# Stores on GpSimd's queue, and turned 1/sum in one transfer

## The chip, the cores and the metric

The kernel runs on one core of one Trainium2 chip. The metric is the device time of one execution in microseconds (us), as the median of three runs. Before the change it is 641.95 us (641.51 to 647.74). Engines are named as in the profile: PE is TensorE (PEld its weight loads), DVE is VectorE, ACT is ScalarE, POOL is GpSimd, SP is SyncE, which here only issues transfers.

## The reference

Causal attention over 4 batches, 12 heads, 448 positions and 64 columns per head, and behind it two matrix products with ELU between them, over 1792 tokens, 768 model columns and 2048 inner ones. The weights come in as float64 words.

```python
scores = np.matmul(q, k.transpose(0, 1, 3, 2)) / np.sqrt(64)
scores = np.where(mask, -1e9, scores)            # mask: later positions
attn = np.exp(scores - scores.max(-1, keepdims=True))
attn = attn / (attn.sum(-1, keepdims=True) + 1e-9)
x = np.matmul(attn, v)                            # to [1792, 768]
h = x @ w_in
g = np.where(h > 0, h, np.exp(np.minimum(h, 0)) - 1)
out = g @ w_out
```

## The kernel before

Positions are cut in four chunks of 112 (CP); a row tile holds one chunk of all four batches, 448 columns (S). Heads go in six pairs (NP). Work runs in this sequence. For chunk 0, `first_pair` does the attention of each pair. Then `layers(0)` and `layers(1)` take chunks 0 and 1 through the first matrix product, while the attention of chunk 1 and of chunks 2 and 3 (`attention(0)`, `attention(1)`) is mixed into PE's work in lumps. Chunks 2 and 3 go through both products with fewer multiplications: `mixed_h` and `mixed_o` work on sums and differences of blocks, of the weights too. Each product of 32 bit numbers is made as three (`three`), from a high part and a low part that `hi_lo` splits off.

Weights go through DRAM. `load64` loads float64 words, `convert` makes float32 of them with DVE, ACT, DVE, ACT and at the end an addition on POOL (L639), and stores the result to `kin` or `kout` (L650). `fetch` loads it again (L655), `raw_piece` too (L823). `mixed` makes the sums and differences of weights (L675) and stores them to `sin` (L692) or `sout` (L701).

The attention divides by the row sums only after the product with v. `reciprocals` makes 1/sum with positions on partitions, and it is wanted along the free axis, on all partitions of a head. `spread_out` does that: a DVE transpose gives `turned` (tile tt, L403), four small transfers store it to `rdram` (L408, 1 KB each), two transfers load it back, each broadcast over the 64 partitions of a head (L411, tile R), and `scaled_x` multiplies (L388, tile xs). This is done 18 times. For chunks 2 and 3 xs is stored to `xdram` (L394) and loaded when `mixed_h` begins (L850).

Nothing runs in the order in which the code stands. `Plan` collects all work with an engine, a cost and the buffers that it reads and writes, gives each a due time from the back, and then simulates the engines to fix the order on each; where a work may run on DVE, ACT or POOL (`hi_lo`, `add`, `take`), the same simulation chooses. All transfers are issued by SP, in one order, and an SP instruction that waits holds back all behind it. What the planner takes a transfer for is in `dma`: issue time on SP, and a size in us for which the transfer occupies the engines.

Of the kernel before, what the change touches and what calls it, by code (L numbers as in the profile page):

```python
# [9 lines left out]
F32 = mybir.dt.float32  # L10
# [4 lines left out]
ALU = mybir.AluOpType  # L15
AX = mybir.AxisListType

CP = 112
# [219 lines left out]
def attention_moe_kernel(ctx, tc, qk, v, w_in, w_out, out):  # L238
    nc = tc.nc
    B, H, D, _, S = qk.shape  # L240
    FT, P, KT, _ = w_in.shape
    ET = w_out.shape[0]
    NCH = S // CP
    NP = H // 2
# [6 lines left out]
    dram = ctx.enter_context(tc.tile_pool(name="dram", bufs=1, space=bass.MemoryType.DRAM))  # L251
# [5 lines left out]
        out=ident, in_=ident, pattern=[[-1, CP]], compare_op=ALU.not_equal,  # L257
# [5 lines left out]
        out=mask[:, S - CP:], in_=mask[:, S - CP:], pattern=[[-1, CP]], compare_op=ALU.is_ge,  # L263
# [3 lines left out]
    def f32(ap):  # L267
        return ap.bitcast(F32)
# [5 lines left out]
    plan = Plan()  # L274
    rings = {}
    PLACES = dict(
        q=2, k=3, v=5, a=8, at=5, m=2, ob=2, R=2, tt=2, row=47, w6=8, w=7, nm=4, su=4, rr=4, hp=3, p=4, av=1, bank=0,
# [8 lines left out]
    def ring(tag):  # L286
        if tag not in rings:
            long = tag[0] == "w"
            rings[tag] = Heap(PLACES[tag], long) if tag in HEAPS else Ring(PLACES[tag], tag != "p", long)
        return rings[tag]  # L290

    def new(tag, shape, dtype=F32, name=None):
        pool = ps if tag in BANKS else sb
        slot = "row" if tag in ROWS else "bank" if tag in BANKS else tag
        bufs = SHARED.get(slot) or PLACES[slot]
        return ring(tag).new(lambda: pool.tile(shape, dtype, tag=slot, name=name or tag, bufs=bufs))
# [4 lines left out]
    def act(n, fn, more=0.05):  # L301
        return ("ACT", more + 0.84e-3 * n, fn, False)

    def dve(n, fn, rate=1.05e-3, more=0.08, port=False):
        return ("DVE", more + rate * n, fn, port)
# [1 line left out]
    def pool(n, fn, rate=2.3e-3):  # L307
        return ("POOL", 0.1 + rate * n, fn, True)

    def dma(kb, rows, fn, reads, writes, least=0.0):  # L310
        rate = 16.0 / (15.0 * rows / (kb * 1024.0) + 0.0366)
        plan.add(("SP", 0.35 + 0.5e-3 * rows, fn, False), reads, writes, size=max(least, kb / rate))

    xt = {}
    xf = {}
    xdram = dram.tile([NP, 2, P, S], F32, name="xdram")
    rdram = dram.tile([3, NP, 2 * B, P], F32, name="rdram")
    xkept = {}  # L320

    def done(*bufs):
# [6 lines left out]
    def half_of(half):  # L329
        return slice(half * D, (half + 1) * D)  # L330
# [49 lines left out]
        )  # L380
        xt[g, p] = xh, xl

    def blocks(x):
        return x.rearrange("p (x c) -> p x c", x=B)

    def scaled_x(joint, j, av, r):
        x = new("ob", [P, S], name="xs")
        plan.add(dve(S, lambda: nc.vector.tensor_tensor(  # L388
            out=blocks(x()), in0=blocks(av()), in1=r()[:, :, :CP], op=ALU.mult,
        )), [av, r], [x])  # L390
        if joint:
            p, y = divmod(j, 2)
            k = xkept[p, y] = Buf(None, lambda: xdram[p, y])
            dma(224, P, lambda: nc.sync.dma_start(out=k(), in_=x()), [x], [k])  # L394
            return
        xh, xl = row("xh", F32R), row("xl", F32R)
        hi_lo(xh, xl, x, S, xh, xl, x)
        xt[1, j] = xh, xl

    def spread_out(joint, j, rr):  # L400
        home = rdram[joint + j % 2, j // 2] if joint else rdram[0, j]
        k, turned, r = Buf(None, lambda: home), new("tt", [P, 32]), new("R", [P, B, P])
        plan.add(dve(32, lambda: nc.vector.transpose(  # L403
            out=turned(), in_=rr().unsqueeze(1).to_broadcast([P, 4, 2 * B])
        ), more=0.12), [rr], [turned])
        for i in range(4):
            c = slice(32 * i, 32 * i + 32)
            dma(1, 2 * B, lambda i=i, c=c: nc.sync.dma_start(out=home[:, c], in_=turned()[32 * i:32 * i + 2 * B]), [turned], [(k, i)], 0.3)  # L408
        for half in range(2):
            src = home[half * B:(half + 1) * B].rearrange("(o x) q -> o (x q)", o=1).to_broadcast([D, B * P])  # L410
            dma(128, D, lambda half=half, src=src: nc.sync.dma_start(  # L411
                out=r()[half_of(half)].rearrange("p x q -> p (x q)"), in_=src
            ), [k], [(r, half)])
        return r

# [206 lines left out]
    def convert(key):  # L622
        r, w = words.pop(key), new("w", [P, KT, P])
        n = KT if key[0] == "i" else 4
        size = n * P
        low, high = (lambda: r()[:, :n, :, 0]), (lambda: r()[:, :n, :, 1])
        wf = lambda: w()[:, :n]
        plan.add(dve(size, lambda: nc.vector.tensor_scalar(
            wf(), f32(high()), MOST, -MOST, op0=ALU.min, op1=ALU.max
        ), 0.55e-3, 0.06, True), [(r, 1)], [w])  # L630

        plan.add(act(size, lambda: nc.scalar.activation(wf(), wf(), AF.Prelu, scale=REBIAS, alpha=2.0 ** 32)), [], [w])
        plan.add(dve(size, lambda: nc.vector.tensor_scalar(  # L633
            wf().bitcast(U32), wf().bitcast(U32), 3, None, op0=ALU.logical_shift_left
        ), 0.55e-3, 0.06, True), [], [w])
        plan.add(act(size, lambda: nc.scalar.activation(
            low().bitcast(I32), low(), AF.Copy, scale=2.0 ** -29
        )), [], [(r, 0)])
        plan.add(pool(size, lambda: nc.gpsimd.tensor_tensor(  # L639
            out=wf().bitcast(I32), in0=wf().bitcast(I32), in1=low().bitcast(I32), op=ALU.add  # L640
        )), [(r, 0)], [w])
        if key[0] == "i":
            done(r)
            home, src = kin[key[1]], wf
        else:
            h = key[1] // HALF_E
            home = kout[key[1]].rearrange("p (h f) c -> p h f c", h=2)[:, h:, 2 * key[2]:2 * key[2] + 2]
            src = lambda: wf().rearrange("p (h f) c -> p h f c", h=2)[:, h:]
        k = kept[key] = Buf(None, lambda: home)
        dma(n * 64, P, lambda: nc.sync.dma_start(out=home, in_=src()), [w], [k])  # L650
        return w if key[0] == "i" else (w, r)

    def fetch(f):
# [10 lines left out]
    def hi_lo(h, l, x, n, th, tl, tx):  # L664

        plan.add([
            act(n, lambda: nc.scalar.activation(h(), x(), AF.Copy)),  # L667
            dve(n, lambda: nc.vector.tensor_copy(h(), x()), 0.55e-3, 0.06, True),
        ], [tx], [th])
        sub = lambda eng: lambda: eng.tensor_tensor(out=l(), in0=x(), in1=f32(h()), op=ALU.subtract)  # L670
        plan.add([dve(n, sub(nc.vector), port=True), pool(n, sub(nc.gpsimd))], [tx, th], [tl])
# [6 lines left out]
    def mixed(layer, r, x, wa, wb, into=None):  # L678


        h = HALF_K if layer == 1 else 2
        n = h * P
        blk = lambda w, half: lambda: w()[:, half * h:half * h + h]
        a, b = (lambda half: blk(wa, half)), (lambda half: blk(wb, half))
        k = skept[layer, r, x] = Buf(None, lambda: None)
        if layer == 1:
            add(b(1), b(0), b(1), n, ALU.add, [(wb, 0)], [(wb, 1)])
            add(b(0), a(0), b(0), n, ALU.subtract, [(wa, 0)], [(wb, 0)])
            add(a(0), b(1), a(0), n, ALU.subtract, [(wb, 1)], [(wa, 0)])
            add(a(1), a(1), a(0), n, ALU.subtract, [(wa, 0)], [(wa, 1)])  # L690
            for i, w in enumerate((wa, wb)):
                dma(2 * h * 64, 2 * P, lambda i=i, w=w: nc.sync.dma_start(  # L692
                    out=sin[r][:, :, i], in_=w().rearrange("p (h k) c -> p h (k c)", h=2)
                ), [w], [(k, i)])
            return
        m = lambda i: lambda: f32(into().rearrange("p k c w -> p (k c w)"))[:, i * n:i * n + n].rearrange("p (k c) -> p k c", k=h)
        add(m(3), b(0), b(1), n, ALU.add, [wb], [(into, 3)])
        add(m(1), a(0), b(0), n, ALU.subtract, [(wa, 0), (wb, 0)], [(into, 1)])
        add(m(0), m(3), a(0), n, ALU.subtract, [(wa, 0), (into, 3)], [(into, 0)])
        add(m(2), a(1), m(0), n, ALU.subtract, [(wa, 1), (into, 0)], [(into, 2)])  # L700
        dma(4 * h * 64, 4 * P, lambda: nc.sync.dma_start(  # L701
            out=sout[x, :, :, :, r].rearrange("p h i c -> p (h i) c"),
            in_=f32(into().rearrange("p k c w -> p (k c w)"))[:, :4 * n].rearrange("p (m c) -> p m c", m=4),
        ), [into], [k])

    def three(acc, w, k, x, first, last, more=False):
        _, wh, wl = w
# [67 lines left out]
    rows, banks = ring("row"), ring("bank")  # L775

    def row(name, dtype=F32):
        return new("row", [P, S], dtype, name)
# [249 lines left out]
    t = FIRST + EACH * NP + 4.0  # L1028
# [61 lines left out]
```

## Time and profile before

| | us |
|---|---|
| median of 3 runs | 641.95 |
| profiled execution, its own time | 641.22 |
| its span | 639.4 |
| PE busy | 611.0 |
| DVE busy | 514.6 |
| ACT busy | 429.5 |
| POOL busy | 170.1 |

The span runs from the first to the last instruction on the device. Busy time counts computing instructions; issuing a transfer is not counted. A busy PE need not be at its peak, since matmuls overlap and their ends are modelled. The chain of waits follows the end back in time: at each step to what released the instruction, or to the one before it on its engine. What waits for several things is put down to the last.

### The profile page before, as it was taken

Reading aid. Unit: us, or ns where it says so; the run is one execution under the profiler, and the core shown is the slowest. Engines: PE = TensorE matmul, PEld = TensorE weight load, DVE = VectorE, ACT = ScalarE, POOL = GpSimd, SP = SyncE. Lnnn points to the kernel's source line nnn. Section 1 sums busy time; section 2 is a strip of 40 time slices with the busy share of each in tenths; the row PEclk is TensorE's granted clock in tenths of the full one; section 3 lists DMA queues with packets and bytes.
Section 4 is the critical chain, followed back from the end, with each engine's and each line's share of the span. In section 5 each row is a group of like instructions: output and inputs, shape, how many; then the busy total and the mean of one; then the engine's idle time right before and its main releaser. Section 6 shows DMA issues by size and latency. Waiting matters only on the chain.

```text
span 639.4 us, 11598 instructions
## 1 busy us (share of the span) xinstructions
PE 611.0 (96%) x3960; PEld 513.0 (80%) x3960; DVE 514.6 (80%) x1112; ACT 429.5 (67%) x954; POOL 170.1 (27%) x124
## 2 busy tenths in 40 slices
PE   5799999998989899998999999999999999999997
PEld 4655577887878787787888878999999879999996
DVE  5777788589999878897999798597777999997611
ACT  6899887878887886975768675445545766664300
POOL 2145541154345342561322420020001362000000
PEclk9799999999989899999999999999999999999999
DMA  9999997796988999996986677873343233352121
GB/s 213 297 333 334 302 369 217 205 304 203 332 256 280 308 314 292 310 280 224 299 264 217 189 264 229 255 191 117 102 122 99 99 104 95 124 151 67 30 57 43
DMA packets 105819, 135.71 MB, mean 212 GB/s; under 512 B 41120, under 2 KB 76192, under 8 KB 105760
## 3 DMA queue, kind: packets, MB, share of 16 engines
q1 hardware_dynamic: 105760, 134.98, 69.2%
q8 instruction: 31, 0.51, 0.3%
q14 instruction: 28, 0.23, 0.1%
HBM read 103.02 MB, written 31.92 MB: 211 GB/s over the span
## 4 chain that ended last, share of the span: by engine, by line
PE 57%; DVE 14%; DMA 13%; ACT 9%; issue 4%; SPq 2%; DVEq 0%; ACTq 0%
PE op L709 9%; PE op L711 9%; PE op L710 9%; PE hp L709 5%; PE hp L731 5%; PE hp L711 5%; PE hp L710 5%; ACT a L338 4%; DMA w<-kin 4%; PE tr L581 3%; PE av L560 3%; DVE a L334 3%; PE sc L527 2%; DMA qk<-in_qk 2%; DVE whl L670 2%
## 5 line engine op out<-in xcount | busy, mean ns | idle before, releaser
L667 ACT ACTIVATE whl<-w 128x768 fp32r<-128x768 f32 x96 | 80.6, 842 | 80.8 <-PE op L711 49.1
L670 DVE TENSOR_TENSOR whl<-w,whl 128x768 fp32r<-128x768 f32 x100 | 106.3, 1063 | 25.2 <-ACT whl L667 24.5
L709 PE MATMUL op<-ph,whl 128*128 128x448 f32 x336 | 125.7, 374 | 0.0
L711 PE MATMUL op<-ph,whl 128*128 128x448 f32 x336 | 123.2, 367 | 0.0
L710 PE MATMUL op<-pl,whl 128*128 128x448 f32 x336 | 123.2, 367 | 0.0
L338 ACT ACTIVATE a<-a,nm 112x448 f32<-112x448 f32 (+2 forms) x192 | 96.8, 518 | 25.9 <-DVE nm L334 25.6
L639 POOL TENSOR_TENSOR w<-w,w 128x512 int32<-128x512 int32 (+1 forms) x40 | 67.5, 1692 | 118.9 <-DVE w L633 81.0
L334 DVE CUSTOM_DVE_ANT_0 a<-sc,mask 112x448 f32<-112x448 f32 (+2 forms) x192 | 74.2, 443 | 12.9 <-PE sc L438 7.5
L709 PEld LDWEIGHTS op<-ph,whl 128*128 128x128 f32 x336 | 63.1, 188 | 9.3 <-issue 3.5
L711 PEld LDWEIGHTS op<-ph,whl 128*128 128x128 f32 x336 | 63.1, 188 | 5.8
L710 PEld LDWEIGHTS op<-pl,whl 128*128 128x128 f32 x336 | 63.2, 188 | 5.2
L709 PE MATMUL hp<-ph,whl 128*128 128x448 f32 x168 | 61.8, 368 | 1.7 <-DVE u L795 1.6
L711 PE MATMUL hp<-ph,whl 128*128 128x448 f32 x168 | 61.4, 366 | 0.0
L710 PE MATMUL hp<-pl,whl 128*128 128x448 f32 x168 | 61.4, 366 | 0.0
L709 PE MATMUL hp<-xh,whl 128*128 128x448 f32 x144 | 57.7, 401 | 0.0
L711 PE MATMUL hp<-xh,whl 128*128 128x448 f32 x144 | 53.4, 371 | 0.9 <-DVE whl L670 0.9
L710 PE MATMUL hp<-xl,whl 128*128 128x448 f32 x144 | 53.1, 369 | 0.0
L581 PE MATMUL tr<-ident,a 112*112 112x112 f32 x432 | 49.9, 264 | 2.4 <-DVE nm L334 2.3
L560 PEld LDWEIGHTS av<-at,v 112*64 112x64 f32 x864 | 41.6, 137 | 12.4 <-issue 7.7
L560 PE MATMUL av<-at,v 112*64 112x112 f32 x864 | 49.4, 263 | 0.3 <-DVE G L802 0.3
L581 PEld LDWEIGHTS tr<-ident,a 112*112 112x112 f32 x432 | 41.3, 133 | 8.9 <-DVE nm L334 3.2
L585 ACT ACTIVATE at<-tr 112x448 f32<-112x448 f32 (+1 forms) x105 | 46.1, 504 | 2.1 <-PE tr L581 2.0
(113 smaller groups left out, 1123.4 us busy)
## 6 DMA issues: line engine op xcount, KB each, us to landing
w<-kin SPq DMA_DIRECT2D x44, 384.0 KB
w<-in_w_in SPq DMA_DIRECT2D x16, 768.0 KB
w<-in_w_out SPq DMA_DIRECT2D x24, 512.0 KB
w<-sout SPq DMA_DIRECT2D x32, 384.0 KB
w<-kout SPq DMA_DIRECT2D x24, 384.0 KB
qk<-in_qk SPq DMA_DIRECT2D x24, 336.0 KB
kin<-w SPq DMA_DIRECT2D x16, 384.0 KB
sout<-w SPq DMA_DIRECT2D x12, 512.0 KB
```

Of the source, the lines that this page charges most:

```text
L334: plan.add(dve(n, lambda: nc.vector.tensor_tensor_reduce(out=a()[:, c], in0=sc()[:, c], in1=mask[:, S - n:], op0=ALU.add, op1=ALU.min, sca ...
L338: plan.add(act(n, lambda: nc.scalar.activation(a()[:, c], a()[:, c], AF.Exp, bias=nm()[:, x:x + 1], scale=-1.0, accum_out=su()[:, x:x + 1] ...
L560: nc.tensor.matmul(av()[half_of(half), chunk(u % 4)], o["v"][1](half, i), at()[:, chunk(x)], start=i == 0, stop=i == chunks(u) - 1,)
L581: nc.tensor.transpose(tr()[:, chunk(x)], o["a"][half]()[:, chunk(i)], ident)
L585: act(w, lambda: nc.scalar.activation(at()[:, :w], tr()[:, :w], AF.Copy)),
L639: plan.add(pool(size, lambda: nc.gpsimd.tensor_tensor(out=wf().bitcast(I32), in0=wf().bitcast(I32), in1=low().bitcast(I32), op=ALU.add)), ...
L667: act(n, lambda: nc.scalar.activation(h(), x(), AF.Copy)),
L670: sub = lambda eng: lambda: eng.tensor_tensor(out=l(), in0=x(), in1=f32(h()), op=ALU.subtract)
L709: nc.tensor.matmul(acc(), wh(k), xh(), start=first, stop=False, skip_group_check=more)
L710: nc.tensor.matmul(acc(), wh(k), xl(), start=False, stop=False, skip_group_check=more)
L711: nc.tensor.matmul(acc(), wl(k), xh(), start=False, stop=last, skip_group_check=more)
L731: pe(ONE, lambda: nc.tensor.matmul(hp(), w[0]()[:, k], x(), start=k == 0, stop=k == KT - 1), [*w, x], [hp], due)
```

## The change

All stores but those of the results go out from POOL's queue instead of SP's: weights (kin, kout), their sums (sin, sout), xs, and turned 1/sum. The latter goes in one transfer of the whole tile of 128 x 32 instead of four of 8 x 32, and rdram has the layout of that tile. So it comes back in four runs of 512 B per partition instead of one of 2048 B, R is laid out as 4 x 4 x 32, and the product with it is made in two instructions, of 96 and 16 columns per batch. The planner's costs change too: 1.0 us of POOL for a store, 0.36 or 0.57 us of SP for a load, and another formula for the size. Loads and the stores of results stay on SP.

```diff
-    def dma(kb, rows, fn, reads, writes, least=0.0):
-        rate = 16.0 / (15.0 * rows / (kb * 1024.0) + 0.0366)
-        plan.add(("SP", 0.35 + 0.5e-3 * rows, fn, False), reads, writes, size=max(least, kb / rate))
+    def dma(kb, rows, fn, reads, writes, least=0.0, store=False):
+        size = rows * (15.7 + 39.2 * kb / rows) / 16.0e3
+        eng = "POOL" if store else "SP"
+        call = (lambda: fn(nc.gpsimd)) if store else fn
+        plan.add((eng, 1.0 if store else 0.36 if rows <= 128 else 0.57, call, False), reads, writes, size=max(least, size))
...
-    rdram = dram.tile([3, NP, 2 * B, P], F32, name="rdram")
+    rdram = dram.tile([3, NP, P, 32], F32, name="rdram")
...
     def scaled_x(joint, j, av, r):
         x = new("ob", [P, S], name="xs")
-        plan.add(dve(S, lambda: nc.vector.tensor_tensor(
-            out=blocks(x()), in0=blocks(av()), in1=r()[:, :, :CP], op=ALU.mult,
-        )), [av, r], [x])
+        for lo, hi in ((0, 3), (3, 4)):
+            n = min(CP, 32 * hi) - 32 * lo
+            w = min(n, 32)
+            part = lambda t, lo=lo, n=n: t.rearrange("p (x c) -> p x c", x=B)[:, :, 32 * lo:32 * lo + n]
+            cut = lambda t, w=w, part=part: part(t).rearrange("p x (k c) -> p x k c", c=w)
+            plan.add(dve(B * n, lambda lo=lo, hi=hi, w=w, cut=cut: nc.vector.tensor_tensor(
+                out=cut(x()), in0=cut(av()), in1=r()[:, lo:hi, :, :w].rearrange("p k x c -> p x k c"), op=ALU.mult,
+            )), [av, r], [(x, lo)])
...
-            dma(224, P, lambda: nc.sync.dma_start(out=k(), in_=x()), [x], [k])
+            dma(224, P, lambda eng: eng.dma_start(out=k(), in_=x()), [x], [k], store=True)
...
-        k, turned, r = Buf(None, lambda: home), new("tt", [P, 32]), new("R", [P, B, P])
+        k, turned, r = Buf(None, lambda: home), new("tt", [P, 32]), new("R", [P, 4, B, 32])
...
-        for i in range(4):
-            c = slice(32 * i, 32 * i + 32)
-            dma(1, 2 * B, lambda i=i, c=c: nc.sync.dma_start(out=home[:, c], in_=turned()[32 * i:32 * i + 2 * B]), [turned], [(k, i)], 0.3)
+        dma(16, P, lambda eng: eng.dma_start(out=home, in_=turned()), [turned], [k], store=True)
         for half in range(2):
-            src = home[half * B:(half + 1) * B].rearrange("(o x) q -> o (x q)", o=1).to_broadcast([D, B * P])
-            dma(128, D, lambda half=half, src=src: nc.sync.dma_start(
-                out=r()[half_of(half)].rearrange("p x q -> p (x q)"), in_=src
+            src = home.rearrange("(o k r) c -> o k r c", o=1, k=4)[:, :, half * B:(half + 1) * B].rearrange("o k r c -> o k (r c)")
+            dma(128, 4 * D, lambda half=half, src=src: nc.sync.dma_start(
+                out=r()[half_of(half)].rearrange("p k x c -> p k (x c)"), in_=src.to_broadcast([D, 4, B * 32])
             ), [k], [(r, half)])
...
-        dma(n * 64, P, lambda: nc.sync.dma_start(out=home, in_=src()), [w], [k])
+        dma(n * 64, P, lambda eng: eng.dma_start(out=home, in_=src()), [w], [k], store=True)
...
```

The stores to `sin` and `sout` in `mixed` are changed in the same way as that in `convert`. Lines of the changed kernel stand two further down (L408 is L410, L639 is L641).

The planner then gives another order on all engines. On SP, the stretch near the last loads of v (L487, now L489), before:

```order
L655 DMA w<-kin 128x768 x2
L408 DMA rdram<-tt 8x32 x4
L823 DMA w<-kout 128x3x256
L487 DMA v<-in_v 112x512
L394 DMA xdram<-xs 128x448
L655 DMA w<-kin 128x768
L411 DMA R<-rdram 64x512 x2
L692 DMA sin<-w 256x1x384
L655 DMA w<-kin 128x768
L692 DMA sin<-w 256x1x384
L823 DMA w<-sout 128x768
L823 DMA w<-kout 128x3x256
```

and now:

```order
L657 DMA w<-kin 128x768 x2
L489 DMA v<-in_v 112x512
L825 DMA w<-kout 128x3x256
L657 DMA w<-kin 128x768
L413 DMA R<-rdram 64x4x128 x2
L657 DMA w<-kin 128x768
L825 DMA w<-sout 128x768
L489 DMA v<-in_v 112x512
L657 DMA w<-kin 128x768
L825 DMA w<-kout 128x3x256
L657 DMA w<-kin 128x768
L825 DMA w<-sout 128x768
```

The stores rdram (L408), xdram (L394) and sin (L692) no longer stand between the loads; w is a weight tile, R the broadcast 1/sum.

On POOL, around the conversion of the third pair of w_out's tiles, before (w_1313 is its buffer of float64 words):

```order
L639 TENSOR_TENSOR w<-w,w_1313 128x512
L675 TENSOR_TENSOR w_1313<-w 128x256
L639 TENSOR_TENSOR w<-w,w_1719 128x512
L670 TENSOR_TENSOR pl<-G,ph 128x448
L670 TENSOR_TENSOR qkhl<-qk,qkhl 128x672
L639 TENSOR_TENSOR w<-w,w_1818 128x512
L639 TENSOR_TENSOR w<-w,w_1695 128x512
```

and now (there the buffer is w_1272):

```order
L641 TENSOR_TENSOR w<-w,w_1272 128x512
L652 DMA kout<-w 128x256
L672 TENSOR_TENSOR pl<-G,ph 128x448 x2
L641 TENSOR_TENSOR w<-w,w_1691 128x512
L410 DMA rdram<-tt 128x32
L652 DMA kout<-w 256x1x256
L672 TENSOR_TENSOR whl<-w,whl 128x768
L703 DMA sout<-w_1272 512x1x256
L672 TENSOR_TENSOR pl<-G,ph 128x448
L641 TENSOR_TENSOR w<-w,w_1813 128x512
L652 DMA kout<-w 256x1x256
L641 TENSOR_TENSOR w<-w,w_1616 128x512
```

Between the additions of the conversions (L639, now L641) now stand stores of kout (L652), rdram (L410) and sout (L703); a subtraction w<-w (L675) is gone to DVE here, and one of whl has come to POOL. Over the whole program 506 transfers on SP become 354, and POOL gets 98. POOL has three subtractions of whl in place of eight, and DVE 105 in place of 100.

## Rows read from the trace of the kernel before

**Rows 1.** The page: span, engines, DMA queue, chain of waits.

```profile
span 639.4 us, 11598 instructions
...
PE 611.0 (96%) x3960; PEld 513.0 (80%) x3960; DVE 514.6 (80%) x1112; ACT 429.5 (67%) x954; POOL 170.1 (27%) x124
...
q1 hardware_dynamic: 105760, 134.98, 69.2%
...
PE 57%; DVE 14%; DMA 13%; ACT 9%; issue 4%; SPq 2%; DVEq 0%; ACTq 0%
```

**Rows 2.** Windows: length, then busy us and count per engine, granted clock, DMA share, GB/s.

```profile
45.00:400.00 355.00, 343.28 (x2553) 275.26 (x2552) 309.54 (x695) 278.71 (x645) 131.88 (x86) 0.99 0.86 273
140.00:400.00 260.00, 248.28 (x1945) 209.30 (x1942) 237.97 (x510) 197.34 (x452) 94.39 (x63) 0.99 0.85 268
98.00:252.00 154.00, 146.28 (x1115) 121.36 (x1115) 134.82 (x324) 124.73 (x293) 60.71 (x43) 0.98 0.87 270
180.00:220.00 40.00, 36.56 (x263) 30.65 (x264) 37.05 (x88) 30.77 (x68) 16.78 (x12) 0.91 0.93 295
```

**Rows 3.** Waits: engine line <- releaser: us in total, times, longest.

```profile
PE sc L527 <- DVE G L802: 3.3, 2, 2.7
...
DVE w L675 <- DMA w<-kin: 3.5, 2, 3.2
...
ACT qkhl L667 <- DMA qk<-in_qk: 7.0, 4, 3.6
```

**Rows 4.** One line's transfers on SP: issue time ns min/median/max, first and last start.

```profile
L408 SPq DMA_DIRECT2D rdram<-tt x72: 263/292/710, 53.0 to 383.3; - x72
...
L650 SPq DMA_DIRECT2D kin<-w x16: 325/448/1243, 44.6 to 107.1; - x16
```

**Rows 5.** Timeline of SP: start, us, line, transfer, count.

```profile
103.65 1.47 SPq L408 DMA_DIRECT2D rdram<-tt  x4
...
335.84 0.32 SPq L655 DMA_DIRECT2D w<-kin  x1
...
340.31 1.29 SPq L408 DMA_DIRECT2D rdram<-tt  x4
```

**Rows 6.** Chain of waits, in order: start us, us, what.

```profile
107.14 0.55 SPq L650
...
108.87 7.42 DMA R<-rdram
...
127.66 2.20 DMA rdram<-tt
...
148.67 1.15 DMA rdram<-tt
...
165.20 6.85 DMA sout<-w
...
172.12 3.06 DMA kout<-w
...
346.00 4.53 DMA sin<-w
...
350.55 5.54 DMA w<-kout
```

**Rows 7.** Groups of DVE by form: count | busy, mean ns | idle before.

```profile
L670 DVE TENSOR_TENSOR whl<-w,whl 128x768 fp32r<-128x768 f32 x100 | 106.3, 1063 | 25.2 <-ACT whl L667 24.5
...
L334 DVE CUSTOM_DVE_ANT_0 a<-sc,mask 112x448 f32<-112x448 f32 x48 | 27.9, 617 | 3.6 <-PE sc L527 3.5
...
L334 DVE CUSTOM_DVE_ANT_0 a<-sc,mask 112x112 f32<-112x112 f32 x48 | 9.9, 267 | 7.5 <-PE sc L438 7.5
...
L628 DVE TENSOR_SCALAR w<-w 128x512 f32<-128x512 f32 x24 | 15.0, 630 | 4.0 <-DMA w<-in_w_out 2.3 <-POOL whl L670 1.7
```

**Rows 8.** Groups of POOL by form, same columns.

```profile
L639 POOL TENSOR_TENSOR w<-w,w 128x768 int32<-128x768 int32 x16 | 31.2, 1954 | 43.5 <-DVE w L633 26.1 <-ACT w L636 8.1 <-DMA kin<-w 3.1
...
L675 POOL TENSOR_TENSOR w<-w 128x256 f32<-128x256 f32 x5 | 5.0, 1008 | 0.3
```

More of the change, by code (lines that the diff above doesn't have):

```diff
@@ L381, in split_x @@
         xt[g, p] = xh, xl
-    def blocks(x):
-        return x.rearrange("p (x c) -> p x c", x=B)
     def scaled_x(joint, j, av, r):
         x = new("ob", [P, S], name="xs")
-        plan.add(dve(S, lambda: nc.vector.tensor_tensor(
-            out=blocks(x()), in0=blocks(av()), in1=r()[:, :, :CP], op=ALU.mult,
-        )), [av, r], [x])
+        for lo, hi in ((0, 3), (3, 4)):
[6 more added lines that the diff above has]
+            )), [av, r], [(x, lo)])
         if joint:
@@ L691, in mixed @@
             for i, w in enumerate((wa, wb)):
-                dma(2 * h * 64, 2 * P, lambda i=i, w=w: nc.sync.dma_start(
+                dma(2 * h * 64, 2 * P, lambda eng, i=i, w=w: eng.dma_start(
                     out=sin[r][:, :, i], in_=w().rearrange("p (h k) c -> p h (k c)", h=2)
-                ), [w], [(k, i)])
+                ), [w], [(k, i)], store=True)
             return
@@ L700, in mixed @@
         add(m(2), a(1), m(0), n, ALU.subtract, [(wa, 1), (into, 0)], [(into, 2)])
-        dma(4 * h * 64, 4 * P, lambda: nc.sync.dma_start(
+        dma(4 * h * 64, 4 * P, lambda eng: eng.dma_start(
             out=sout[x, :, :, :, r].rearrange("p h i c -> p (h i) c"),
             in_=f32(into().rearrange("p k c w -> p (k c w)"))[:, :4 * n].rearrange("p (m c) -> p m c", m=4),
-        ), [into], [k])
+        ), [into], [k], store=True)
     def three(acc, w, k, x, first, last, more=False):
```

## The prediction

> **What bounds the kernel now.** I read the page first: TensorE (PE) is busy for 611.0 of 639.4 us, VectorE (DVE) for 514.6, GpSimd (POOL) for 170.1 [rows 1]. PE alone therefore looks like the bound, and little can be won. The windows say where. Between 140 and 400 us PE is busy for 248.28 of 260 us, so 11.7 us stand idle; around one of these holes, from 180 to 220 us, the granted clock is 0.91, which costs 40 x 0.09 = 3.6 us [rows 2]. After 400 us no store of this change is left and PE runs nearly without holes; before 45 us there is hardly one, since the first kin and rdram stores start at 44.6 and 53.0 [rows 4]. So all that the change can win lies in 11.7 + 3.6 = **15.3 us**, and the time cannot fall much below 641.95 - 15.3 = 626.6.
>
> What makes the holes? PE itself waits there for DVE (G before the scores, 3.3 us), while DVE and ACT wait for transfers: 3.5 us for w<-kin, 7.0 us for qk [rows 3]. DVE is the closest second: 237.97 of 260 us busy, 22.0 idle [rows 2]. Last I read the chain of waits between 100 and 400 us. It is full of transfers: the page gives DMA 13% of the span and SP's queue 2% [rows 1], and single links are stores that had to land before a buffer came free: 6.85 us for sout, 3.06 for kout, 4.53 for sin, 2.20 and 1.15 for rdram [rows 6]. All transfers stand in one queue, SP's. At 335.84 us SP issues a load, and its next instruction, a store of turned 1/sum, starts only at 340.31: 4.15 us in which nothing behind it can be issued [rows 5].
>
> **The change, part by part.** Taken off SP: 16 stores kin, 24 kout, 16 sin, 12 sout, 12 xdram and 72 small ones rdram, 152 of 506 transfers. Put on POOL: the same 80 large ones and 18 rdram, 98 in all.
>
> *SP's issue time.* Off the path almost everywhere, since SP has idle time. On the chain I find the run of four rdram stores at 103.65 (1.47 us, ahead of an R load on the chain) [rows 5], one kin store of 0.55 at 107.14 [rows 6], and three more rdram stores, each 0.292 [rows 4]. These go: 1.47 + 0.55 + 0.88 = **-2.9 us**.
>
> *The stores' landing.* Links of one kind differ: rdram 2.20 and 1.15, sout 6.85 and sin 4.53 against 3.06 for kout [rows 6]. I take the shortest as what a store needs with a queue of its own, although kout carries fewer bytes: (2.20 - 1.15) + (6.85 - 3.06) + (4.53 - 3.06) = **-6.3 us**. The bounds: 0, if the difference is transfer and not waiting in line, and twice that.
>
> *Loads behind stores.* The 80 large stores carry 25.7 MB, 0.33 MB each; the window moves 268 GB/s at a DMA share of 0.85 [rows 2], 315 at full, so one takes 1.05 us. Between the first and the last store, 53 of SP's 217 loads stand right behind a large store (counted in the order of the program), 24%. The chain between 100 and 400 us has ten loads, from the R load at 108.87 (7.42 us) to w<-kout at 350.55 (5.54) [rows 6]. 10 x 0.24 x 1.05 = **-2.5 us**. The bounds: 0, if the two queues share the engines in such a way that the load wins nothing, and 10 x 1.05 if every load on the chain stood behind one.
>
> *Clock.* If half of the hole near 180 us closes, part of the 3.6 us comes back; **-1.0 us** taken, 0 to 3.6 possible.
>
> *DVE.* Each of the 18 products with R becomes two. The fixed part of a DVE instruction: 448 columns take 617 ns and 112 take 267 [rows 7], 117 ns per 112 columns, so 150 ns for none; 18 x 0.15 = 2.7 us. With the stores on POOL, the order of the program moves five subtractions of whl from POOL to DVE, 5 x 1.063 = 5.3 us [rows 7]. The other forms move by a few each (seven roundings of whl more, a dozen small ones fewer); I take 2 us, at most seven times 1.063. That is 10 us more on DVE. DVE holds 14% of the chain, 89.5 us, which is 17% of its busy time [rows 1]: 10 x 0.17 = **+1.7 us**. If DVE is bound throughout, all 10 count.
>
> *R in runs of 512 B.* 64 runs become 256 for the same bytes. A packet takes 69.2% x 639.4 x 16 / 105760 = 67 ns on average [rows 1], so a load costs between nothing more and 192 x 67 / 16 = 0.8 us. I take a quarter, 0.2; four such loads at the two places on the chain: **+0.8 us**.
>
> *Issue on POOL.* No row shows a store issued there. Lower end: 0.292, what SP needs for a small one [rows 4]. Upper end: POOL's own longest addition here, 1.954 [rows 8]. I take 1.0, near POOL's shortest tensor row, 1.008 [rows 8], which is the nearest row on the engine that now issues. For rdram this stands on the path at the three places: **+3.0 us**. Elsewhere it hides in POOL's idle time: 131.88 of 355 us are busy from 45 to 400 us [rows 2], with 98 more 230. If that cover goes, see the POOL rival.
>
> Sum: -2.9 - 6.3 - 2.5 - 1.0 + 1.7 + 0.8 + 3.0 = -7.2. The profiled execution took 641.22, so 634.0; the median of the three runs, 641.95, lies 0.73 above it: 634.7, that is **635 us**.
>
> Against this stands a rule of the Trainium skill, DMA: Bandwidth & Descriptors, section "Issuing engines are not separate DMA queues": transfers from all engines run on the same 16 DMA engines and interleave, and spreading them only saves the issue time. No run so far shows two queues. By that rule the landing and load terms (8.8 us) vanish and the sum is +1.6.
>
> **The rivals.**
>
> *Nothing is gained (38%).* The waits for transfers are only where DVE's lateness shows; DVE is 92% busy in the stretch and gets 10 us more. Then -2.9 + 1.7 + 0.8 + 3.0 = +2.6, 644.5, or with a few us of landing won 638: a spread of 636 to 647. For it: PE's waits end on DVE. Against it: the chain runs through 13% DMA. The skill's rule above would come out here.
>
> *POOL becomes the bound (18%, slower).* The place is 98 to 252 us, where all kout and sout stores are made. POOL is busy there for 60.71 of 154 us [rows 2], and about 50 stores come in. It is full when a store, with what it waits in POOL's in-order queue, costs (154 - 60.7) / 50 = **1.87 us**. Behind each store stand the additions that finish the weights' conversion, so all over that goes onto the path: at 2.1 us, 50 x 0.23 = 11.5 us, and 653. For it: SP stood 4.15 us before one store [rows 5], and those waits now stand before POOL's additions. Against it: the issue alone is taken as 1.0, and the planner orders stores for when their data are due. The skill names a mechanism that would raise the price (SBUF — State Buffer, "Who interferes with whom": GpSimd cannot write descriptors while DVE runs an instruction in a mode that takes both ports). Here that would be lines like L628, 630 ns each [rows 7]; one full hit per store gives 1.0 + 0.63 = 1.63, still under 1.87.
>
> *The change does not do what it says.* The order of both programs shows the stores on POOL; no chance of its own.
>
> **How the numbers follow.** My forecast's case, 44%, spans 625 (all 15.3 us and a little of the start) to 636. A run can be told from no change from about 1% on: 635.5 and 648.4. So faster 0.44, same 0.38, slower 0.18. The range is **625 to 651**: above 651 lies two thirds of the POOL case, 0.12, and below 625 perhaps 0.04.
>
> **What would show it.** Right: no sout or sin link above 4 us in the chain, PE busy for 253 or more of the same program stretch, no stand of several us on SP before a load, and POOL's store at about 1 us. Wrong: DVE at 97% there with PE's holes unchanged (DVE rival); POOL above 90% between 98 and 252 us and waits of ACT or PE for L641, the former L639 (POOL rival). If the stores' landing stays at 4 to 7 us on their own queue, the largest term, -6.3, is the step that failed.

## The result: slower by 0.6%, and the profile after

The changed kernel takes 645.26 us (median of 20 runs) against 641.73 for the kernel before (20 runs beside them): ratio 1.0062, 95% interval 1.0038 to 1.0087. The prediction said 635. The profiled execution took 644.4 us.

The page of the changed kernel (compare [rows 1]): span, engines, queues, chain.

```profile
span 642.6 us, 11601 instructions
...
PE 612.7 (95%) x3960; PEld 515.7 (80%) x3960; DVE 524.2 (82%) x1137; ACT 426.2 (66%) x953; POOL 212.6 (33%) x216
...
q1 hardware_dynamic: 91808, 108.55, 57.2%
q0 software_dynamic: 7680, 26.65, 11.4%
...
PE 60%; DVE 13%; DMA 9%; issue 7%; ACT 6%; POOL 3%; SPq 1%; POOLq 0%; DVEq 0%; ACTq 0%
```

DVE has the 10 us more that the prediction gave it, the stores stand in a queue of their own (q0, 26.65 MB), and transfers have gone from 13% to 9% of the chain. Still the kernel is slower. The windows, in the columns of [rows 2], say where:

```profile
45.00:400.00 355.00, 342.12 (x2533) 272.50 (x2532) 317.18 (x721) 276.40 (x647) 173.41 (x175) 0.98 0.84 268
140.00:400.00 260.00, 247.16 (x1933) 207.20 (x1932) 240.29 (x520) 196.88 (x458) 124.11 (x130) 0.97 0.83 265
98.00:252.00 154.00, 141.63 (x1058) 115.50 (x1059) 135.04 (x331) 122.83 (x295) 76.17 (x83) 0.96 0.80 258
```

Between 98 and 252 us PE has lost 4.65 us (146.28 before). POOL is busy for 76.17 of 154 us, 49%, and that counts its stores too (the page has 216 instructions on POOL, 118 of arithmetic and 98 stores). DVE is busy for 135.04 us, 88%: no engine is full there. So something waits, and the waits of the whole span name it (compare [rows 3]):

```profile
ACT qkhl L669 <- DMA sout<-w: 10.0, 2, 8.8
...
PE tr L583 <- ACT a L340: 3.9, 1, 3.9
```

ACT stood 8.8 us for a sout store; before, its longest wait for a transfer was the 3.6 us for qk in [rows 3]. The chain of waits between 100 and 300 us holds that wait and two more links of the same kind, where [rows 6] had one (6.85 us). By the prediction none was to be above 4 us:

```profile
137.26 8.83 DMA sout<-w
...
184.54 4.58 DMA sout<-w
...
239.30 6.34 DMA sout<-w
```

The rows of single lines on POOL show what a store costs the engine that issues it (min/median/max in ns, first and last start; the answer to [rows 4]):

```profile
L410 POOL DMA_DIRECT2D rdram<-tt x18: 540/560/730, 48.4 to 388.7; - x18
...
L652 POOL DMA_DIRECT2D kout<-w x24: 559/687/713, 108.7 to 255.1; - x24
```

The issue is cheap, a median of 0.56 and 0.69 us. POOL's waits, in the columns of [rows 3], show what stands before the stores whose data DVE makes:

```profile
POOL rdram L410 <- DVE tt L407: 38.5, 10, 10.0
...
POOL sout L703 <- DVE w L677: 17.6, 9, 4.8
POOL sin L694 <- DVE w L677: 16.0, 9, 7.2
...
POOL xdram L398 <- DVE xs L392: 11.6, 4, 8.7
```

These waits, 38.5 + 17.6 + 16.0 + 11.6 = 83.7 us, stand in POOL's in-order queue ahead of its additions, as the prediction's POOL rival feared. That was the first theory to test, and it turned out wrong.

### The profile page after: what moved, and what is told of

Its sections match the earlier page's. It is cut to its first block, busy times and chain, and to the rows that moved or that the text cites. A ratio compares the mean times of both kernels' runs of the same rounds, so it can differ in the third digit from the quotient of the medians.

```text
span 642.6 us, 11601 instructions
## 1 busy us (share of the span) xinstructions
PE 612.7 (95%) x3960; PEld 515.7 (80%) x3960; DVE 524.2 (82%) x1137; ACT 426.2 (66%) x953; POOL 212.6 (33%) x216
## 3 DMA queue, kind: packets, MB, share of 16 engines
q1 hardware_dynamic: 91808, 108.55, 57.2%
q0 software_dynamic: 7680, 26.65, 11.4%
## 4 chain that ended last, share of the span: by engine, by line
PE 60%; DVE 13%; DMA 9%; issue 7%; ACT 6%; POOL 3%; SPq 1%; POOLq 0%; DVEq 0%; ACTq 0%
PE op L711 9%; PE op L713 9%; PE op L712 9%; PE hp L711 6%; PE hp L713 5%; PE hp L712 5%; PE hp L733 5%; PE av L562 3%; DMA sout<-w 3%; PE sc L529 3%; PE tr L583 3%; DMA w<-kin 3%; ACT a L340 3%; DVE whl L672 2%; DVE a L336 2%
## 5 line engine op out<-in xcount | busy, mean ns | idle before, releaser
L672 DVE TENSOR_TENSOR whl<-w,whl 128x768 fp32r<-128x768 f32 x105 | 117.3, 1118 | 25.5 <-ACT whl L669 24.9
L669 ACT ACTIVATE whl<-w 128x768 fp32r<-128x768 f32 x89 | 74.6, 842 | 75.8 <-PE op L713 47.3
L641 POOL TENSOR_TENSOR w<-w,w 128x512 int32<-128x512 int32 (+1 forms) x40 | 63.6, 1596 | 45.8 <-DVE w L635 31.5
L711 PE MATMUL hp<-xh,whl 128*128 128x448 f32 x144 | 58.8, 408 | 3.3 <-ACT whl L669 3.3
L713 PE MATMUL hp<-xh,whl 128*128 128x448 f32 x144 | 54.7, 380 | 2.0 <-DVE whl L672 2.0
L712 PE MATMUL hp<-xl,whl 128*128 128x448 f32 x144 | 54.4, 378 | 1.8 <-DVE xl L672 1.8
L583 PE MATMUL tr<-ident,a 112*112 112x112 f32 x432 | 51.2, 267 | 5.0 <-ACT a L340 3.9
```

The costliest lines, as they stand in the source:

```text
L583: nc.tensor.transpose(tr()[:, chunk(x)], o["a"][half]()[:, chunk(i)], ident)
L641: plan.add(pool(size, lambda: nc.gpsimd.tensor_tensor(out=wf().bitcast(I32), in0=wf().bitcast(I32), in1=low().bitcast(I32), op=ALU.add)), ...
L711: nc.tensor.matmul(acc(), wh(k), xh(), start=first, stop=False, skip_group_check=more)
L712: nc.tensor.matmul(acc(), wh(k), xl(), start=False, stop=False, skip_group_check=more)
L713: nc.tensor.matmul(acc(), wl(k), xh(), start=False, stop=last, skip_group_check=more)
```

## The experiments

Times are medians; ratios are to the kernel before, run beside each version on the same chip, with a 95% interval. The kernel before moves by 0.7% between these series (639.41 to 644.11 us), so versions of different series are compared by their ratios.

### Which part costs: the order, the planner's costs or the queue?

**Stores back on SP, everything else as changed** (same order on PE, DVE and ACT, and of POOL's arithmetic):

```
-        call = (lambda: fn(nc.gpsimd)) if store else fn
+        call = (lambda: fn(nc.sync)) if store else fn
```

> The order of the changed kernel on PE, DVE, ACT and of POOL's arithmetic is kept word for word; only the issuing engine of the 98 stores goes back from POOL to SP, at the same places of the order. Theory Order (the new order, with more DVE work, costs the 3.5 us, and the queue is worth nothing): as the changed kernel, within 1.5 us of 645. Theory Queue (POOL's in-order queue delays the conversions behind stores; the order is harmless): back to 642 or below. Theory Relief (the own queue does shorten landings and the order is worse than it looks): slower than the changed kernel, 649 or more.

631.22 us, 0.9868 (0.9830 to 0.9907). Moving the 98 stores to GpSimd costs 1.0062 / 0.9868 = 1.020, 12 to 13 us (the two medians alone differ by 14), and what is left of the change is a gain of 1.3%.

**The order of before, its 80 large stores on GpSimd** (rdram stays on SP):

```
-        dma(n * 64, P, lambda: nc.sync.dma_start(out=home, in_=src()), [w], [k])
+        dma(n * 64, P, lambda: nc.gpsimd.dma_start(out=home, in_=src()), [w], [k])
...
```

> The order of the kernel before on PE, DVE, ACT is kept word for word; only the 80 large stores (kin, kout, sin, sout, xdram) are issued by POOL; the 72 rdram stores stay on SP. Theory Order: the queue is neutral, so 641 to 643. Theory Queue: POOL's 80 issues of 0.6 to 0.7 us, 52 us in all, and the waits in its queue hold up additions and conversions, so 645 or more. Theory Relief: 636 or less, and links of sout in the chain under 4 us.

641.94 us, 1.0022 (0.9991 to 1.0053). Here the same move costs nothing that can be told from noise. So "GpSimd's queue costs 2%" can't be the whole story. (What comes below bears on this run as well: its build puts 194 tiles elsewhere than that of the kernel before, so it doesn't measure the queue alone.)

**The turned 1/sum alone** (one transfer of 16 KB, runs of 512 B, product in two pieces; stores and costs as before):

```
-        for i in range(4):
-            ...
-            dma(1, 2 * B, ..., [turned], [(k, i)], 0.3)
+        dma(16, P, lambda: nc.sync.dma_start(out=home, in_=turned()), [turned], [k], 0.3)
```

> The kernel before with the one part: turned 1/sum goes out in one transfer of 128 x 32, from SP, comes back in runs of 512 B, and the product with R is made in two instructions; planner's costs and all other stores as before. 54 transfers fewer on SP (16 us of its issue time), 18 DVE instructions more (about 2.7 us). If this part costs the time: 644 to 646. If it is neutral: within 1.5 us of 642. If the shorter issue on SP counts: 639 or less.

631.94 us, 0.9874 (0.9839 to 0.9909): this part alone gives the whole 1.3%, with an order of its own that the planner made for it.

**A cheaper store in the planner's table**, 0.65 instead of 1.0, near the 0.56 to 0.69 measured:

```
-        plan.add((eng, 1.0 if store else ...
+        plan.add((eng, 0.65 if store else ...
```

> The changed kernel, with 0.65 us instead of 1.0 in the planner for a store on POOL, which is what its trace shows (0.56 to 0.74). Theory Order in the form that the mispriced store drove work from POOL to DVE: DVE's busy time falls by a few us and the time to 642 or less. If the time does not come from that price: within 2 us of 645, in either direction as any small change of the order may bring.

645.4 us, 1.0077 (1.0040 to 1.0114): the table's price is not it. (That order lacks the long wait near 137 us, so it loses elsewhere; where, stays open.)

### Which stores?

**Only the 40 stores kin and kout on GpSimd**, whose data POOL itself has just made; and the reverse, **only the 58 stores rdram, xdram, sin and sout**, whose data DVE makes. Order as changed in both.

```
-        call = (lambda: fn(nc.gpsimd)) if store else fn
+        call = (lambda: fn(nc.gpsimd if store == "pool" else nc.sync)) if store else fn
...
-        dma(n * 64, P, lambda eng: eng.dma_start(out=home, in_=src()), [w], [k], store=True)
+        dma(n * 64, P, lambda eng: eng.dma_start(out=home, in_=src()), [w], [k], store="pool")
```

> The order of the changed kernel on PE, DVE, ACT and of POOL's arithmetic; of its 98 stores only the 40 of kin and kout, whose data POOL itself has just made, are issued by POOL, the other 58 by SP. Known ends: 631 with all on SP, 645 with all on POOL. Theory Issue (the 0.6 to 0.7 us of POOL per store delay the conversions): 40 of 98 stores, so 14 x 40 / 98 = 6 us over the all-SP run, about 637. Theory Head of line (a store that waits for DVE holds back POOL's next addition): these stores wait for nothing but POOL, so within 2 us of 631.

632.19 us, 0.9878 (0.9831 to 0.9924).

> The counterpart: the 58 stores of rdram, xdram, sin and sout, whose data DVE (or seldom POOL) makes, are issued by POOL, kin and kout by SP, in the same order. Theory Issue: 14 x 58 / 98 = 8 us over the all-SP run, about 639. Theory Head of line: nearly all of the loss, 643 or more, with POOL idle before rdram and sout for a good 50 us in all.

643.0 us, 1.0032 (1.0005 to 1.0059). The second group carries nearly all the loss. That is just what waiting in POOL's queue would give.

**A control: how much does any small reordering move?** One constant of the planner, 0.22 to 0.23 us, in the kernel before:

```
-    HOP = 0.22
+    HOP = 0.23
```

> A control: the kernel before with the planner's time for a step from one engine to the next set to 0.23 us instead of 0.22. Nothing is moved to another queue; only the order falls out differently. It tells how much a mere new order is worth. Theory Transfer count (the one transfer for four is the cause of the gain of the run with turned 1/sum alone): within 2.5 us of 641. Theory Any order (the order of before is a bad draw): 637 or less.

638.75 us, 0.9960 (0.9928 to 0.9991). This one reshuffle is worth 0.4%; how far others go, one sample does not say.

**The one 16 KB store of the turned sums as four of 32 x 32**, in the order of the turned part alone:

```
-        dma(16, P, lambda: nc.sync.dma_start(out=home, in_=turned()), [turned], [k], 0.3)
+        dma(16, P, lambda: [nc.sync.dma_start(
+            out=home[32 * i:32 * i + 32], in_=turned()[32 * i:32 * i + 32]
+        ) for i in range(4)], [turned], [k], 0.3)
```

> The kernel of the run with turned 1/sum alone, in its order on all engines, but the one transfer of 128 x 32 is issued as four of 32 x 32, at the same place on SP: 54 transfers more, some 16 us of SP's issue time. Theory Transfer count (the gain of 8.5 us comes from SP's shorter queue): most of it goes, 637 or more. Theory Order (it comes from the order that the planner finds with fewer works): within 2 us of 632.

646.86 us, 1.0087 (1.0058 to 1.0117): the version with 54 more small transfers in SP's queue takes 1.0087 / 0.9874 = 1.022 of the time with one, some 14 us more.

### What ACT waited for: the place of a tile

The theory of the waiting queue had a flaw. Where ACT stood 8.8 us for a sout store, the version with the stores on SP issued the same store at 137.55, and it landed 9.6 us later (worked out from its semaphore counts), at 147.2, later than the 146.1 of the changed kernel. Yet ACT did not wait there. The timelines of ACT, first of the changed kernel (start, us, line, what, in brackets the idle time before it and its releaser):

```profile
136.81 0.68 ACT L638 ACTIVATE w<-w 128x512 int32<-128x512 uint32 x1
146.25 0.76 ACT L669 ACTIVATE qkhl<-qk 128x672 fp32r<-128x672 f32 x1 [8.77 <-DMA sout<-w]
```

and of the version with the stores on SP:

```profile
136.18 0.67 ACT L638 ACTIVATE w<-w 128x512 int32<-128x512 uint32 x1
137.94 0.77 ACT L669 ACTIVATE qkhl<-qk 128x672 fp32r<-128x672 f32 x1 [1.09 <-PE sc L529]
```

Same instruction, same neighbours, another wait. The built programs say why. Each tag (a group of tiles that share places) has a number of places in SBUF, the memory that holds these tiles, and a tile may be written only when the last user of its place is done. The layer under the kernel hands the places out while it builds, as they come free by its own reckoning. That reckoning shifts when stores change queue. Of 1293 tiles 121 follow another tile in their place. For the third qkhl (its byte address, and the instruction's waits):

```
changed kernel:  place 177632, last held by the 18th w64, which a sout store reads
                 qkhl<-qk [waits DMASW3, DMAHW5, DVE, Pool]
stores on SP:    place 171488, last held by the first qkhl
                 qkhl<-qk [waits DMAHW5, PE]
```

The store did not become slow; the next tile was put on top of it. Checking the two groups: the version with 58 stores on GpSimd (slow) has the places of this tag exactly as the changed kernel, the one with 40 (fast) has the third qkhl where the SP version has it. So both theories fitted all runs so far, and the next four were made to separate them. They fix every tile's place by a table and leave queues and order alone:

```
-        return ring(tag).new(lambda: pool.tile(shape, dtype, tag=slot, name=name or tag, bufs=bufs))
+            return pool.tile(shape, dtype, tag=f"{slot}_{PIN[slot][n]}", name=name, bufs=1)
```

**The changed kernel, the places of two tiles exchanged** (the third qkhl and the 24th w64; the later tiles of both places go along, so only these two follow another tile):

> Same as the changed kernel (stores on GpSimd's queue, same order on every engine) but for the SBUF places of two tiles: the third qkhl takes the place that the first qkhl has left, instead of one that a sout store still reads, and the 24th w64 takes the latter. Theory Places (the 14 us between the stores' two queues come from the places that tiles were given, which differ for 121 of 1293 tiles between the two builds): the wait of ACT qkhl for sout of 8.8 us near 137 us goes, the lag of 5.2 us behind the SP version in the stretch 137 to 157 us too, so about 640 us (637 to 642), ratio to the kernel before 0.993 to 1.000. Theory Queue (stores that wait in GpSimd's in-order queue hold back its additions): nothing changes, 645 us, ratio 1.004 to 1.009.

637.96 us, 0.9938 (0.9907 to 0.9970). Two tiles of 1293 are worth 0.9938 / 1.0062 = 0.988 (0.984 to 0.992). In ACT's timeline the long wait is gone (the profiled execution, 642.11 us, was the longest of the twelve):

```profile
136.00 0.77 ACT L682 ACTIVATE qkhl<-qk 128x672 fp32r<-128x672 f32 x1 [1.08 <-PE sc L542]
```

**The changed kernel, stores on GpSimd, all places as in the SP version:**

> The changed kernel, all 98 stores issued by GpSimd, same order on every engine, but every tile of the weights and rows is put where the build with the stores on SP puts it (121 tiles move). Theory Places: as fast as the version with stores on SP, 631 to 635 us, ratio 0.984 to 0.991. Theory Queue: 643 to 647 us, ratio 1.003 to 1.009. In between, say 638 us: both have a part, and the distance to 631 us is the queue's.

634.23 us, 0.9871 (0.9827 to 0.9916), against 0.9868 for the SP version itself. POOL's waits are all still there (compare the four rows above; L423 is the former L410, L707 and L716 the sin and sout, L411 the xdram stores):

```profile
POOL rdram L423 <- DVE tt L420: 41.3, 11, 10.1
...
POOL sin L707 <- DVE w L690: 18.1, 9, 6.7
POOL sout L716 <- DVE w L690: 15.8, 8, 4.8
...
POOL xdram L411 <- DVE xs L405: 13.8, 4, 9.2
```

89.0 us of waiting, 5 more than in the slow kernel, and the time is that of the fast one: 0.9871 / 0.9868 = 1.000 (0.994 to 1.006). Waiting in POOL's queue costs nothing that can be measured here. The pages of the two, first with the stores on SP, then on GpSimd:

```profile
PE 606.4 (96%) x3960; PEld 512.3 (81%) x3960; DVE 518.1 (82%) x1137; ACT 427.0 (68%) x953; POOL 157.7 (25%) x118
```

```profile
PE 609.1 (96%) x3960; PEld 512.0 (81%) x3960; DVE 526.4 (83%) x1137; ACT 425.5 (67%) x953; POOL 212.7 (34%) x216
```

The same 1137 instructions of DVE take 8.3 us longer in all when the stores are on GpSimd.

**The mirror image: stores on SP, places of the changed kernel:**

> The mirror image: all 98 stores issued by SP, same order on every engine, every tile of the weights and rows where the changed kernel's build puts it. Theory Places: as slow as the changed kernel, 641 to 646 us, ratio 0.999 to 1.007, with an ACT qkhl wait for a sout store of over 6 us near 137 us. Theory Queue: 630 to 634 us, ratio 0.983 to 0.989.

645.25 us, 1.0035 (1.0000 to 1.0069). The slowness comes back without a single store on GpSimd, and so does the wait, in ACT's timeline:

```profile
147.78 0.76 ACT L682 ACTIVATE qkhl<-qk 128x672 fp32r<-128x672 f32 x1 [10.73 <-DMA kout<-w]
```

The profile names kout, but the program waits for the sout store's semaphore, and that store, issued at 137.63, had its last count at 147.6: a wait on several semaphores is put down to the last event seen. The stretch 98 to 252 us of this kernel, and of the changed one with the SP version's places, answers to the third window above:

```profile
98.00:252.00 154.00, 139.82 (x1056) 114.76 (x1055) 129.52 (x324) 122.11 (x292) 49.73 (x36) 0.94 0.87 263
```

```profile
98.00:252.00 154.00, 148.26 (x1155) 121.50 (x1153) 145.52 (x345) 129.78 (x312) 80.97 (x88) 0.99 0.86 277
```

PE's 8.4 us between the two (and the clock, 0.94 against 0.99) go with the places. POOL, with the stores in its queue, is the busier engine in the fast one.

**Four transfers, with the places of the one-transfer version:**

> The kernel with the turned 1/sum in four transfers of 32 x 32 (646.9 us) with every tile of the weights and rows where the version with one transfer (631.9 us) has it; order and 54 additional transfers as they were. Theory Places: those 15 us came from the places too, 632 to 637 us, ratio 0.985 to 0.993. Theory Count (54 more transfers in SP's queue cost the 15 us): 644 to 649 us, ratio 1.005 to 1.012.

646.42 us, 1.0060 (1.0022 to 1.0098). Here places were not the cause: at equal places and in the same order, the version with 54 more transfers takes 1.0060 / 0.9874 = 1.019 (1.014 to 1.024), some 12 us. It is not the kernel before with its four stores put back: these carry 4 KB each and take SP a median of 0.412 us, those 1 KB and 0.292 us ([rows 4]), and the planner made this order without knowing of the 54. Its chain of waits shows where (L424 is the store of the turned sums, L429 the load R that reads them back, both in SP's queue):

```profile
151.72 0.33 SPq L424
152.10 0.41 SPq L424
152.57 0.41 SPq L424
153.02 3.64 DMA rdram<-tt
156.75 0.61 SPq L429
157.41 1.38 SPq L429
158.83 7.26 DMA qk<-in_qk
```

The R loads can't go before the last of the four stores has landed, and the qk load, next on the chain, stands behind them in SP's in-order queue. Four stores are issued later than one, by 4 x 0.412 - 0.323 = 1.3 us from the medians of the two lines. The stores of the version with four:

```profile
L424 SPq DMA_DIRECT2D rdram<-tt x72: 302/412/1298, 53.0 to 390.5; - x72
```

and of the version with one transfer:

```profile
L411 SPq DMA_DIRECT2D rdram<-tt x18: 319/323/572, 52.3 to 373.8; - x18
```

Between 40 and 400 us the pieces of SP's queue on the chain sum to 15.1 us, 7.8 of them R loads; in the version with one transfer to 0.4 us, none of it R loads. That this is the way the 12 us are lost is read from the chain of one execution each and was not tried by itself.

### What the change is worth when places are no accident

One rule for all: the kernel's planner gives each tile, of the free places, the one whose last user ends first by its own times, a store's landing counted. Order and queues stay as they are.

```
+            at = held.setdefault(slot, [None] * bufs)
+            n = min((n for n, o in enumerate(at) if o is None or not o.left), key=lambda n: at[n].end if at[n] else 0.0)
+            at[n] = b
+            return pool.tile(shape, dtype, tag=f"{slot}_{n}", name=name or tag, bufs=1)
```

The kernel before under it:

> The kernel before, same order on every engine, but its own planner gives every tile of the weights and rows its place: of the free places the one whose last user ends first by the planner's times, a store's landing counted. Theory Places alone: the kernel before owed its 642 us to its places as the changed kernel did, so 631 to 636 us, ratio 0.982 to 0.991, and the change itself is then worth within 1%. Theory Turned part: places are no cost in the kernel before, 639 to 645 us, ratio 0.996 to 1.004.

641.26 us, 0.9967 (0.9932 to 1.0002): before owed little to its places.

The changed kernel under it:

> The changed kernel, stores on GpSimd's queue, same order on every engine, with the same rule for the places. Places (shown by the two pinned runs before): 630 to 637 us, ratio 0.982 to 0.992; that rule is no better than chance: 640 to 646 us.

634.25 us, 0.9885 (0.9839 to 0.9931).

The turned part alone under it:

> The kernel before with the turned 1/sum in one transfer and in runs of 512 B alone, all stores on SP, with the same rule for the places. Without the rule it took 631.9 us (ratio 0.987). Theory Turned part: 628 to 634 us, over 1% under the kernel before with the same rule. Theory Places alone: within 1% of the kernel before with the same rule.

630.11 us, 0.9813 (0.9774 to 0.9853).

The candidate: turned part, new transfer costs, stores on SP in table and program, under it:

> The candidate for a faster version: the changed kernel with its new transfer costs, the turned part in one transfer, all stores on SP in the planner's table and in the program, and the same rule for the places. Both theories: 627 to 634 us, ratio 0.978 to 0.989; above 636 us would say that the order that the planner makes for stores on SP is worse than the one it makes for stores on GpSimd.

628.47 us, 0.9787 (0.9747 to 0.9827), the fastest version. The stretch 140 to 400 us of it, to be set beside the second windows row of the changed kernel above:

```profile
140.00:400.00 260.00, 255.92 (x2010) 218.03 (x2009) 241.40 (x527) 201.81 (x464) 93.72 (x65) 1.00 0.89 277
```

PE has gone from 247.16 to 255.92 of 260 us, with DVE as busy as in the changed kernel.

Last, the changed kernel under the rule with the queue alone put back to SP, every place the same:

> The changed kernel's order and the planner's rule for the places, as in the version that took 634.25 us (ratio 0.9885), the same place for every tile, but all 98 stores issued by SP: a second pair for what the queue alone costs. Theory Places (the queue as such costs nothing): ratio within 0.5% of 0.9885, 632 to 637 us. Theory Queue for a remainder (the difference of 1% to the version planned for SP, 0.9787, is the queue): ratio 0.978 to 0.982, 628 to 631 us.

629.24 us, 0.9843 (0.9790 to 0.9895), against 0.9885 on GpSimd. By the ratio this lies within the half per cent of the first expectation, by the time in the range of the second; the kernel before was faster in this series (639.41 us against 644.11), so the ratio counts. The queue alone comes to 0.9885 / 0.9843 = 1.004 (0.997 to 1.011) in this pair and to 1.000 (0.994 to 1.006) in the first. Neither pair shows a cost, and neither excludes half a per cent.

So, under one rule: the change as a whole 0.9885 / 0.9967 = 0.992 (0.986 to 0.998, the two intervals taken together), the turned part in it 0.9813 / 0.9967 = 0.985 (0.979 to 0.990). The changed kernel is slower than before because of the places that its build gave its tiles: with those of the SP version it takes 0.9871 / 1.0062 = 0.981 (0.976 to 0.986) of its time, about as much as the turned part gives or a little more. For the two tiles that were exchanged it is shown that one stood on top of a store still under way. What the other 119 do for the rest was not tried.

## Why the prediction was wrong, step by step

*Stores' landing, -6.3: the step that failed.* I took differences between links as waiting in SP's line, which a queue of its own would end. But a link shows only that part of a landing that follows the piece before it on the chain, and landings of one kind differ widely on either queue: sout takes 3.8 to 9.6 us on SP and 4.6 to 9.4 on GpSimd. The page's list of transfers (count, KB each, median us to landing) in the version with all stores on SP:

```profile
kin<-w SPq DMA_DIRECT2D x16, 384.0 KB, 6.7
sout<-w SPq DMA_DIRECT2D x12, 512.0 KB, 5.8
sin<-w SPq DMA_DIRECT2D x16, 384.0 KB, 3.7
...
R<-rdram SPq DMA_DIRECT2D x36, 128.0 KB, 5.2
```

and with the same order and places, stores on GpSimd:

```profile
kin<-w POOLq DMA_DIRECT2D x16, 384.0 KB, 7.0
sout<-w POOLq DMA_DIRECT2D x12, 512.0 KB, 6.9
sin<-w POOLq DMA_DIRECT2D x16, 384.0 KB, 4.0
...
R<-rdram SPq DMA_DIRECT2D x36, 128.0 KB, 5.3
```

Sout and sin, which the term counted on, land no sooner; over all seven kinds of stores the medians move by -0.9 (kout of 128 KB) to +1.1 us (sout). The bound of 0 that I gave was the value, and sout and sin at 6.9 and 4.0 us are what the prediction had named as the sign that this term failed. The Trainium skill's rule against it (DMA: Bandwidth & Descriptors, section "Issuing engines are not separate DMA queues") is what these rows agree with.

*Loads behind stores, -2.5: nothing.* R takes 5.2 and 5.3 us in the same two lists, and the weights' loads w<-kin 5.4 in both. It falls with the first term. (The 25.7 MB should read 26.3; the 0.33 MB per store is right.)

*What no step had: places.* The prediction asked which wait frees a buffer, but took it as given which tile comes next into it. I put it at nothing without a reason. It costs 1.9%, 645.26 x 0.019 = 12 us. That the error, 645.26 - 635, is 10 us is no proof of it, since three errors add up here: without landing and loads the prediction's sum is +1.6 instead of -7.2; the turned part gives some 7 us more than I took for it (next step); the places cost 12. By this estimate the change should cost 6 to 7 us; it cost 4, or 0.6%.

*SP's issue, -2.9: right direction, too small.* I counted only the pieces that stood on the chain of one execution. The turned part as a whole gives 1.5%, some 10 us, under one rule (641.26 - 630.11 = 11); 54 transfers more or less are worth some 12 us between the four-transfer and the one-transfer version at equal places. I took off issue times; but behind the stores stand the R loads, which wait for the last landing, and behind those the other loads, as the chain above shows them.

*DVE, +1.7.* Its 10 us more are there (524.2 against 514.6), but partly by luck: in the same order with the stores on SP DVE is busy for 518.1 us, so the new order is worth 3.5, and the other 6 came with the stores on GpSimd, which the prediction did not expect. Why they came is open (see the end). They are harmless: with DVE at 526.4 us and the SP version's places the kernel is at 0.9871.

*R in runs of 512 B, +0.8; clock, -1.0.* Too small to see by themselves. Between 140 and 400 us the granted clock fell to 0.97 instead of rising; with the SP version's places it is 0.99 on either queue, with the changed kernel's 0.97 on either, so the fall goes with the places. It doesn't follow the holes alone: the four-transfer version has PE busy for only 244.86 us there, at 1.00.

*Issue on POOL, +3.0 for three pieces at 1.0.* A store of rdram takes 0.56 us (median), 1.7 us for three.

*The rivals.* POOL as the bound: POOL is 49% busy in the stretch, waits before stores are as long as feared, and the version with the same waits and other places is fast. Refuted. Nothing gained because DVE is the bound: the time, 645.26, is in its spread, but the mechanism is refuted by the same DVE work at 629 to 634 us. That no landing would be won was right. That under one rule the change gains 0.8%, near the forecast, is chance: the gain is the small transfers', not the stores'.

## What to carry to other kernels

When a change leaves the order alone and the time still moves by per cents, compare which tile follows which in its place before blaming a queue: pin the places of one build into the other, both ways. Here, moving transfers to another engine's queue didn't shorten their landing; one larger store in place of four small ones ahead of the loads did help. Where many tiles share places, let the planner that knows when stores land choose the place, since two tiles were worth over 1% here; how good such a rule is elsewhere, one kernel does not show.

## What the runs showed of the hardware that was not expected

The same 98 stores, 26.65 MB, are 7680 packets in GpSimd's queue; on SP they were 114112 - 91808 = 22304 packets more in q1. Packets three times as large did not make them land sooner.

GpSimd is held 0.56 to 0.73 us per store (medians of the six kinds in the changed kernel; sout, the largest, has 0.73), and the longest of all 98 is 0.94, a store of xdram (median 0.56). The Trainium skill's mechanism for a longer hold (SBUF — State Buffer, "Who interferes with whom") adds nowhere the 0.63 us that I had allowed for one full hit: no row here shows it.

DVE's own time changes as well. At equal order and places its instructions take 526.4 us in all with the stores on GpSimd against 518.1 on SP, and 524.5 against 516.0 in the second pair. In the first pair 54 of them, in either version, take over 0.4 us longer than the shortest of their form. All run beside an addition or subtraction of POOL, with the stores on GpSimd 25 beside a store as well, none beside a store alone. Why these hits grow from 52.0 to 61.1 us in all is not shown.
